# Half of a tuned kernel's first layer by seven half-size products in place of eight

## The chip, the cores and the metric

The kernel runs on 1 core of one Trainium2 chip. The metric is the device time of one execution in microseconds (us), median over several runs. The ratios are of runs in the undisturbed state ("fast"), in which the profiler shows 0.992 to 1.0 of TensorE's clock granted.

## The reference

Sliding-window attention (8 batches, 8 heads, 576 positions, head size 64, window 32 to each side), then a two-layer network with a gelu over 4608 tokens:

```python
scores = scale * np.matmul(q, k.transpose(0, 1, 3, 2))
mask = np.abs(pos[:, None] - pos[None, :]) <= 32
attn = softmax(np.where(mask, scores, -1e9))          # cut: written out in the reference
x = np.matmul(attn, v) ...                            # to 4608 x 512
h = x @ w_in                                          # 512 -> 2048
g = h * (1.0 / (1.0 + np.exp(-1.702 * h)))
return (g @ w_out).astype(np.float32)                 # 2048 -> 512
```

## The kernel before

Tokens are worked off in windows of 256. In window w the kernel does attention for its tokens, the first layer for those of window w-1 and the second layer for those of window w-2. Windows 0 to 3 are the head, 4 and 5 lead in, 6 to 17 are alike, 18 and 19 close. The second layer is done already by a product of 2 x 2 blocks with seven block products in place of eight (Strassen's scheme in Winograd's form): VectorE makes the sums of g (`g_sums`) and keeps partial results (`keep`, `result`), TensorE does seven `product`s of 8 matmuls.

The first layer is plain: for each pair of 128-column blocks of w_in, 8 matmuls with 256 tokens as the moving operand, then a gelu on ScalarE.

```python
def layer1(self, t, d, kind="h"):
    hps = self.bank(kind, [128, 2, 256], F32, "h_ps")
    ffs = (d, d + 8) if t > 2 else (2 * d, 2 * d + 1)
    for i in range(2):
        ff = ffs[i]
        for kr in range(self.NK):
            nc.tensor.matmul(hps[:, i, :], self.w_in_sb[:, kr, ff * 128:(ff + 1) * 128], self.xT[t][:, kr, :], ...)
    nc.scalar.activation(self.g[t][:, ffs[0]:ffs[1] + 1:ffs[1] - ffs[0], :], hps, AF.Gelu_apprx_sigmoid)

def window(self, w):                     # cut to the order for w > 5; t = w - 2
    self.scores(a); self.scores(b)
    self.g_sums(t, 1, (0, 1)); self.product(t, 1, "o"); self.keep(t, 1, dve)
    self.product(t, 2, "h"); self.g_sums(t, 1, (2, 3)); self.result(t, 11)
    self.product(t, 5, "t"); self.band(a); self.product(t, 6); self.band(b, 0); self.keep(t, 6, dve); self.band(b, 1)
    run(l1)                              # one layer1
    self.values(a); self.values(b); self.norm(a); self.x_T(a)
    self.product(t, 7); self.keep(t, 7, dve); self.result(t, 22); run(l1, 1)
    self.product(t, 4); self.result(t, 21, act); self.norm(b); self.x_T(b)
    self.product(t, 3); self.result(t, 12)
    run(l1, 2); self.g_sums(w - 1, 0); self.feed(w); run(l1, 4)
```

In the head, vo copies (shifted copies of v that the values need) stand ahead of the masks:

```python
for m in range(4, 7):
    self.odd_v(m, dve)
self.band(4)
```

The softmax here doesn't subtract the row's maximum and nothing guards it: scores larger than these inputs give would overflow.

## Time and profile before

| | before |
|---|---|
| time, median of the first 3 runs | 291.88 us (291.85 to 293.37) |
| TensorE busy | 283.1 us, 98% of the span |
| VectorE, ScalarE busy | 190.5 (66%), 183.3 (63%) |
| one window | 14.57 us |
| VectorE, ScalarE busy in a window | 10.13 to 10.4, 9.87 |

How to read the lines that follow: PE is TensorE, PEld its weight loads, DVE VectorE, ACT ScalarE. A line of the chain of waits is a start and a length in us, the engine, the tile that it writes, the line of the kernel and how many instructions. The tiles are `sc` (scores), `p` (their exponentials), `ve` and `vo` (v and its shifted copies), `pv` (values), `x` (normed values), `tp` (transposes), `h_ps` (plain first layer), `h_main` and `h_side` (the two banks of the seven products, new in the change), `xs` and `wi_sum` (the sums of x and of w_in, also new), `g` (after the gelu), `gs` (sums of g), `o_ps` (second layer), `part` and `o_sb` (its partial and finished results). A bank is one of the pieces of memory in which this kernel's matmuls leave their results. A bracket at the end of a timeline line is the time that the engine stood idle before it, and what ended that.

Read the chain of waits first: the column of starts gives the length of a window, and the names tell that only TensorE stands in it from 46 us until the last results at 284.4. Then ask of the chain's pieces what they are made of, and of VectorE and ScalarE how much room a window leaves them. The prediction shows the lines.

### The profile page before, as it was taken

How to read it: one execution, taken by the hardware profiler on the slowest of the kernel's cores; microseconds unless marked ns; L12 is line 12 of the kernel's file. 1: busy time of each engine (PE TensorE's matmuls, PEld its weight loads, DVE VectorE, ACT ScalarE, POOL GpSimd, SP SyncE). 2: the span in 40 equal slices, each digit the busy share in tenths (PEclk: the TensorE clock that was granted, in tenths of full speed). 3: DMA queues.
4: the chain of work that ended last, by engine and by line, in shares of the span. 5: the costliest groups of instructions: out<-in, count | busy, mean ns of one | idle time of the engine just before them, and what ended most of it. 6: DMA issues, size and time to landing. Idle time of an engine off the chain costs nothing.

```text
span 289.8 us, 9011 instructions
## 1 busy us (share of the span) xinstructions
PE 283.1 (98%) x3757; PEld 233.7 (81%) x3759; DVE 190.5 (66%) x563; ACT 183.3 (63%) x301; POOL 101.7 (35%) x140
## 2 busy tenths in 40 slices
PE   7989999999999999999999999999999999999995
PEld 2668655866888888888888888888888888888884
DVE  6871558679576767676767685858585858583352
ACT  4576366695757676767666666767676767675330
POOL 8854425997635443442524343422000000000000
PEclk9999999999999999999999999999999999999999
DMA  9999999999999999999999999999925220312012
GB/s 152 189 200 205 199 183 161 165 138 150 176 141 151 157 193 139 160 157 162 154 181 111 154 133 160 130 159 137 152 57 147 36 93 20 95 21 91 2 72 72
DMA packets 144824, 38.79 MB, mean 134 GB/s; under 512 B 129936, under 2 KB 140432, under 8 KB 144784
## 3 DMA queue, kind: packets, MB, share of 16 engines
q0 software_dynamic: 97232, 18.16, 85.3%
q1 hardware_dynamic: 47104, 19.67, 38.9%
q8 instruction: 29, 0.48, 0.7%
q10 hardware_dynamic: 448, 0.39, 0.5%
q14 instruction: 11, 0.09, 0.2%
HBM read 36.96 MB, written 9.44 MB: 160 GB/s over the span
## 4 chain that ended last, share of the span: by engine, by line
PE 82%; DMA 12%; POOL 3%; DVE 1%; issue 1%; ACT 0%; POOLq 0%; DVEq 0%
PE h_ps L339 39%; PE o_ps L401 32%; DMA ks<-in_k_dram 5%; DMA ve<-in_v_dram 4%; PE o_ps L351 4%; PE pv L299 4%; PE sc L270 3%; DMA w_in_sb<-in_moe_w_in_dram 3%; POOL ve L159 1%; PE tp L178 1%; POOL ks L137 0%; POOL ks L197 0%; POOL qs L197 0%; PE tp L326 0%; DVE o_sb L419 0%
## 5 line engine op out<-in xcount | busy, mean ns | idle before, releaser
L339 PE MATMUL h_ps<-xT,w_in_sb 128*128 128x256 bf16 x1152 | 134.9, 273 | 0.0
L341 ACT ACTIVATE g<-h_ps 128x512 f16<-128x512 f32 x144 | 85.6, 595 | 73.3 <-PE h_ps L339 72.0
L339 PEld LDWEIGHTS <-w_in_sb 128*128 128x128 bf16 x1152 | 112.1, 98 | 13.4
L159 POOL DMA_DIRECT2D ve<-in_v_dram x41 | 34.4, 849 | 76.2 <-PE pv L299 56.8
L401 PEld LDWEIGHTS <-gs 128*128 128x128 f16 x480 | 45.8, 98 | 5.8
L401 PE MATMUL o_ps<-w_sum,gs 128*128 128x256 f16 x360 | 44.3, 273 | 0.0
L277 ACT ACTIVATE p<-sc 128x512 bf16<-128x512 f32 x72 | 37.2, 604 | 3.8 <-PE sc L270 3.6
L378 DVE TENSOR_TENSOR gs<-g 128x512 f16<-128x512 f16 x30 | 12.8, 425 | 38.5 <-ACT g L341 38.5
L401 PEld LDWEIGHTS <-g 128*128 128x128 f16 x360 | 34.2, 98 | 4.5 <-ACT g L341 0.2
L311 DVE TENSOR_TENSOR x<-pv,rec 128x256 bf16<-128x256 f32 x72 | 30.6, 424 | 2.5
L401 PE MATMUL o_ps<-w_out_sb,g 128*128 128x256 f16 x240 | 29.1, 273 | 0.0
L105 DVE COPY part<-o_ps 128x256 f32<-128x256 f32 x45 | 19.1, 424 | 12.2 <-PE o_ps L401 11.1
L419 DVE TENSOR_TENSOR o_sb<-o_ps,part 128x256 f32<-128x256 f32 x45 | 19.0, 422 | 12.1 <-PE o_ps L401 11.4
L105 DVE COPY vo<-ve 64x528 bf16<-64x528 bf16 x71 | 22.6, 318 | 6.0 <-DMA ve<-in_v_dram 4.4
L288 DVE TENSOR_TENSOR p<-p,mask 128x512 bf16<-128x512 bf16 x64 | 24.6, 425 | 0.7 <-ACT p L277 0.6
L147 POOL DMA_DIRECT2D qs<-in_q_dram x27 | 22.8, 868 | 5.9 <-DMA ks<-in_k_dram 4.8
L147 POOL DMA_DIRECT2D ks<-in_k_dram x27 | 22.8, 858 | 2.7 <-DMA ve<-in_v_dram 1.5
L351 PE MATMUL o_ps<-w_out_sb,g 128*128 128x512 f16 x96 | 23.2, 380 | 0.0
L438 ACT ACT_TABLE_LOAD x15 | 19.2, 1283 | 0.3
L277 ACT ACT_TABLE_LOAD x15 | 19.2, 1283 | 0.3
L310 DVE RECIPROCAL rec<-pv 128x4 f32<-128x4 f32 x72 | 12.5, 174 | 6.2 <-PE pv L299 6.2
L299 PEld LDWEIGHTS <-p 128*64 128x64 bf16 x576 | 11.1, 110 | 6.2 <-DVE p L288 3.9
(79 smaller groups left out, 237.0 us busy)
## 6 DMA issues: line engine op xcount, KB each, us to landing
out_dram<-o_sb SPq DMA_DIRECT2D x34, 256.0 KB, 4.4
ve<-in_v_dram POOLq DMA_DIRECT2D x31, 128.0 KB, 6.1
ks<-in_k_dram POOLq DMA_DIRECT2D x24, 128.0 KB, 7.1
qs<-in_q_dram POOLq DMA_DIRECT2D x24, 128.0 KB, 8.5
w_in_sb<-in_moe_w_in_dram POOLq DMA_DIRECT2D x4, 512.0 KB, 9.2
w_out_sb<-in_moe_w_out_dram POOLq DMA_DIRECT2D x4, 512.0 KB, 14.1
ve<-in_v_dram POOLq DMA_DIRECT2D x10, 64.0 KB, 6.1
ks<-in_k_dram POOLq DMA_DIRECT2D x7, 64.0 KB, 6.0
```

The source lines that it names most:

```text
L105: (eng.copy if eng is self.nc.scalar else eng.tensor_copy)(out, in_)
L147: self.nc.gpsimd.dma_start(self.stage[key][off:off + m, n], src[b, :, s:s + m, :].rearrange("h s d -> s h d"))
L159: self.nc.gpsimd.dma_start(self.ve[m % NV][lo + off:lo + off + n, :, :self.D], self.v[b, :, s:s + n, :].rearrange("h s d -> s h d"))
L277: nc.scalar.activation(p[:, eo], sc[eo], AF.Exp, scale=self.scale)
L288: self.nc.vector.tensor_mul(pv, pv, msk.to_broadcast([128, 4, 2, SQ]))
L299: nc.tensor.matmul(acc[half][blk * 64:blk * 64 + 64, hh, :], p[:, h % 2, h // 2 * 2 + blk, :], vt[:, h, :D + 1], start=(hh == 0), stop=(hh ...
L311: nc.vector.tensor_mul(x[:, hs, :], acc[half][:, :, :D], rec[:, hs, :].to_broadcast([128, 4, D]))
L339: nc.tensor.matmul(hps[:, i, :], self.w_in_sb[:, kr, ff * 128:(ff + 1) * 128], self.xT[t][:, kr, :], start=(i == 0 and kr == 0), stop=(i = ...
L341: nc.scalar.activation(self.g[t][:, ffs[0]:ffs[1] + 1:ffs[1] - ffs[0], :], hps, AF.Gelu_apprx_sigmoid)
L351: nc.tensor.matmul(o_ps, self.g[t][:, ff, s * 128:(s + 1) * 128], self.w_out_sb[:, ff, :], start=(ff == 0), stop=(ff == self.NFF - 1))
L401: nc.tensor.matmul(self.part[t, key], x, y, start=(first and k == 0), stop=(k == 7), skip_group_check=True)
L438: self.nc.scalar.activation(self.spark, self.spark, AF.Gelu_apprx_sigmoid)
```

## The change

The intent is to save matmul columns in the first layer by the scheme that the second layer has. Half of it (column blocks 4 to 7 and 12 to 15) is cut in 2 x 2 blocks, and eight block products become seven, each of 8 matmuls of 128 columns. The operands become f16, since sums of them are taken. The price is sums of x per window, sums of w_in once, and moves between banks, on VectorE and ScalarE. The second layer's sums are placed anew around the masks, pairs of banks are joined so that one mask, one exponential or one norm serves both halves, and a few orders and buffers move.

```diff
+    def w_in_sums(self):                  # once, in window 5
+        dve.tensor_add(ws[:, 0], w[:, top, v], w[:, low, v])
+        dve.tensor_sub(ws[:, 1], ws[:, 0], w[:, top, u])
+        dve.tensor_sub(ws[:, 2], w[:, top, u], w[:, top, v])
+        dve.tensor_sub(ws[:, 3], w[:, low, u], ws[:, 1])
+    def seven(self, t, n):                # 4 blocks x 2 matmuls of 128 columns; cut
+        dst = hs["main" if n in (1, 6, 5, 3) else "side"]
+    def steady(self, w):                  # windows 6 to 17; t = w - 1, o = w - 2; loads and gelu_table cut
+        self.scores(a, which=0); self.scores(b, which=1)
+        self.g_sums(o, 1, (0, 1)); self.product(o, 1, "o"); self.keep(o, 1, dve)
+        self.g_sums(o, 0, (2,)); self.product(o, 2, "t"); self.result(o, 11)      # if w > 6
+        self.product(o, 6); self.band(a); self.keep(o, 6, dve); self.product(o, 5, "t"); self.band(b)
+        self.g_sums(o, 1, (2,)); self.seven(t, 1); self.move("side", "main", dve); self.x_sums(t, (0, 1))
+        self.values(a, which=0); self.values(b, which=1); self.norm(a); self.x_T(a)
+        self.product(o, 7); self.keep(o, 7, dve); self.result(o, 22); self.x_sums(t, (2, 3)); self.norm(b); self.x_T(b)
+        ...                               # two g_sums
+        self.seven(t, 2); self.gelu(t, "side", 0, 0); self.seven(t, 6); self.move("k2", "main", act)
+        self.layer1(t, 0, "a"); self.product(o, 4); self.result(o, 21, act)
+        self.seven(t, 7); self.move("k7", "side", act); self.seven(t, 5); self.move("22", "main", dve, "k7")
+        self.feed(w); self.layer1(t, 1, "b"); self.gelu(t, "22", 1, 1); self.layer1(t, 2, "b"); self.layer1(t, 3, "a")
+        self.seven(t, 4); self.move("21", "side", dve, "k2"); self.seven(t, 3)
+        self.gelu(t, "main", 0, 1); self.gelu(t, "21", 1, 0)
+        self.g_sums(t, 0, (0, 1)); self.product(o, 3); self.result(o, 12)
@@ window
-        if w > 5:
-            self.scores(b)
-        self.product(t, 2, "h")
-        if w == 5:
-            self.scores(b)
+        self.product(t, 2, "h")
+        self.scores(b, which=1)
         self.feed(w)
+        self.w_in_sums()
         run(l1, 4)
@@ head
-        self.keep_busy(2, "h")
+        self.keep_busy(2, "o")            # fillers ahead of scores 2
-        for m in range(4, 7):
+        for m in range(4, 6):
             self.odd_v(m, dve)
         self.norm(4)
+        self.odd_v(6, dve)
-        o_sb ... bufs=4
+        o_sb ... bufs=3
```

More of the change, by code (lines that the diff above doesn't have):

```diff
@@ L59, in __init__, with pair, halves @@
         self.gs, self.part, self.o_sb = {}, {}, {}
+        self.xs, self.hs, self.turn = {}, {}, 0
     def bank(self, kind, shape, dtype, name):
-        bufs = {"h": 2, "o": 1, "a": 4, "t": 1}[kind]
+        bufs = {"h": 2, "o": 1, "t": 1, "b": 2}[kind]
         return self.ps.tile(shape, dtype, name=name, tag=kind, bufs=bufs)
+    def pair(self, name, which=None):
+        if which is None:
+            which, self.turn = self.turn, 1 - self.turn
+        if which == 0:
+            return self.ps.tile([128, 2, 512], F32, name=name, tag="a", bufs=1)
+        return [self.bank("b", [128, 512], F32, f"{name}{i}") for i in range(2)]
+    @staticmethod
+    def halves(pair):
+        return pair if isinstance(pair, list) else [pair[:, i] for i in range(2)]
     def setup(self):
@@ L69, in setup @@
         self.mask = cst.tile([128, 4, SQ], BF16, name="mask")
-        self.w_in_sb = cst.tile([128, self.NK, self.DFF], BF16, name="w_in_sb")
+        self.w_in_sb = cst.tile([128, self.NK, self.DFF], F16, name="w_in_sb")
+        self.wi_sum = cst.tile([128, 4, 2, self.DFF // 4], F16, name="wi_sum")
+        self.ident16 = cst.tile([128, 128], F16, name="ident16")
         self.w_out_sb = cst.tile([128, self.NFF, self.DM], F16, name="w_out_sb")
@@ L214, in load_raw @@
         lo, size = self.tokens("A")
-        raw = self.stage[c, "raw", hp] = self.cst.tile([size // JT, 2, JT * self.D], F32, name=f"{c}_raw{hp}")
+        if "raw" not in self.stage:
+            self.stage["raw"] = self.work.tile([128, 4, 2, JT * self.D], F32, name="raw", tag="gs")
+        raw = self.stage[c, "raw", hp] = self.stage["raw"][:size // JT, 2 * hp + "kq".index(c)]
         src = {"q": self.q, "k": self.k}[c]
@@ L248, in blind, with scores @@
     def blind(self, u):
-        sc = self.sc[u] = [self.bank("a", [128, 8, SQ], F32, f"sc{eo}") for eo in range(2)]
+        sc = self.sc[u] = self.pair("sc")
         neg = self.neg.rearrange("k (o b) s -> k o b s", o=1).to_broadcast([128, 4, 2, SQ])
         for eo in range(2):
-            self.nc.tensor.matmul(sc[eo].rearrange("k (h b) s -> k h b s", b=2), self.ident, neg,
+            self.nc.tensor.matmul(self.halves(sc)[eo].rearrange("k (h b s) -> k h b s", b=2, s=SQ), self.ident, neg,
                                   start=True, stop=False, skip_group_check=True)
-    def scores(self, u):
+    def scores(self, u, which=None):
         nc = self.nc
@@ L259, in scores @@
         if seen:
-            self.sc[u] = [self.bank("a", [128, 8, SQ], F32, f"sc{eo}") for eo in range(2)]
-        sc = self.sc.pop(u)
+            self.sc[u] = self.pair("sc", which)
+        both = self.sc.pop(u)
+        sc = [half.rearrange("k (h s) -> k h s", s=SQ) for half in self.halves(both)]
         k0, q0 = 128 * u % RING, (128 * u + 32) % RING
@@ L275, in scores, with band @@
         p = self.work.tile([128, 2, 8, SQ], BF16, name="p", tag="p", bufs=5)
-        for eo in range(2):
-            nc.scalar.activation(p[:, eo], sc[eo], AF.Exp, scale=self.scale)
+        if isinstance(both, list):
+            for eo in range(2):
+                nc.scalar.activation(p[:, eo], sc[eo], AF.Exp, scale=self.scale)
+        else:
+            nc.scalar.activation(p.rearrange("k e h s -> k e (h s)"), both, AF.Exp, scale=self.scale)
         self.p[u] = p
-    def band(self, u, only=None):
+    def band(self, u):
         p = self.p[u]
@@ L284, in band, with values @@
         a, b = 0 if cross[0] else 1, 2 if cross[1] else 3
-        for eo in range(2) if only is None else (only,):
-            pv = p[:, eo].rearrange("p (h b) s -> p h b s", b=2)
-            msk = self.mask[:, a:b + 1:b - a, :].rearrange("p (o b) s -> p o b s", o=1)
-            self.nc.vector.tensor_mul(pv, pv, msk.to_broadcast([128, 4, 2, SQ]))
-    def values(self, u, kinds="aa"):
+        pv = p.rearrange("p e (h b) s -> p (e h) b s", b=2)
+        msk = self.mask[:, a:b + 1:b - a, :].rearrange("p (o b) s -> p o b s", o=1)
+        self.nc.vector.tensor_mul(pv, pv, msk.to_broadcast([128, 8, 2, SQ]))
+    def values(self, u, kinds=None, which=None):
         nc, D = self.nc, self.D
         p = self.p.pop(u)
-        acc = [self.bank(kinds[i], [128, 4, D + 1], F32, f"pv{i}") for i in range(2)]
+        if kinds is None:
+            both = self.pair("pv", which)
+            acc = [half[:, :4 * (D + 1)].rearrange("q (h d) -> q h d", d=D + 1) for half in self.halves(both)]
+            if isinstance(both, list):
+                self.acc[u] = acc
+            else:
+                self.acc[u] = [both[:, :, :4 * (D + 1)].rearrange("q i (h d) -> q i h d", d=D + 1)]
+        else:
+            acc = self.acc[u] = [self.bank(kinds[i], [128, 4, D + 1], F32, f"pv{i}") for i in range(2)]
         for half in range(2):
@@ L300, in values @@
                                      vt[:, h, :D + 1], start=(hh == 0), stop=(hh == 3))
-        self.acc[u] = acc
     def norm(self, u):
@@ L305, in norm @@
         acc = self.acc.pop(u)
-        x = self.work.tile([128, self.H, D], BF16, name="x", tag="x", bufs=4)
+        x = self.work.tile([128, self.H, D], F16, name="x", tag="x", bufs=4)
         rec = self.work.tile([128, self.H, 1], F32, name="rec", tag="rec", bufs=3)
+        if len(acc) == 1:
+            rec4 = rec.rearrange("q (i h) o -> q i h o", i=2)
+            nc.vector.reciprocal(rec4, acc[0][:, :, :, D:D + 1])
+            nc.vector.tensor_mul(x.rearrange("q (i h) d -> q i h d", i=2), acc[0][:, :, :, :D],
+                                 rec4.to_broadcast([128, 2, 4, D]))
+            self.x[u] = x
+            return
         for half in range(2):
@@ L317, in x_T @@
         if s == 0:
-            self.xT[t] = self.work.tile([128, self.NK, 256], BF16, name="xT", tag="xT", bufs=4)
+            self.xT[t] = self.work.tile([128, self.NK, 256], F16, name="xT", tag="xT", bufs=4)
         x = self.x.pop(u)
@@ L323, in x_T @@
             return
-        tp = self.bank(kind, [128, 4, 128], BF16, "tp")
+        tp = self.bank(kind, [128, 4, 128], F16, "tp")
         for c in range(4):
-            nc.tensor.transpose(tp[:, c, :], x[:, 2 * c:2 * c + 2, :], self.ident)
+            nc.tensor.transpose(tp[:, c, :], x[:, 2 * c:2 * c + 2, :], self.ident16)
         self.cast(eng or nc.vector, out, tp)
@@ L331, in layer1 @@
         nc = self.nc
-        if d == 0:
+        if t not in self.g:
             self.g[t] = self.work.tile([128, self.NFF, 256], F16, name="g", tag="g", bufs=2)
-        hps = self.bank(kind, [128, 2, 256], F32, "h_ps")
+        if kind == "a":
+            hps = self.pair("h_ps", 0)[:, 0].rearrange("p (i s) -> p i s", i=2)
+        else:
+            hps = self.bank(kind, [128, 2, 256], F32, "h_ps")
         ffs = (d, d + 8) if t > 2 else (2 * d, 2 * d + 1)
@@ L353, in layer2 @@
         if quarter == 3:
-            o_sb = self.work.tile([128, self.DM], F32, name="o_sb", tag="o_sb", bufs=4)
+            o_sb = self.work.tile([128, self.DM], F32, name="o_sb", tag="o_sb", bufs=3)
             self.cast(eng or nc.vector, o_sb, o_ps)
@@ L412, in result @@
         if u not in self.o_sb:
-            self.o_sb[u] = self.work.tile([128, self.DM], F32, name="o_sb", tag="o_sb", bufs=4)
+            self.o_sb[u] = self.work.tile([128, self.DM], F32, name="o_sb", tag="o_sb", bufs=3)
         cols = slice(256 * half, 256 * half + 256)
@@ L438, in gelu_table, with keep_busy @@
         self.nc.scalar.activation(self.spark, self.spark, AF.Gelu_apprx_sigmoid)
-    def keep_busy(self, n, kind="a"):
+    def keep_busy(self, n, kind="b"):
         junk = self.bank(kind, [128, 512], F32, "junk")
@@ L456, in head @@
         self.setup_neg()
+        dve.tensor_copy(self.ident16, self.ident)
         for m in range(2):
@@ L498, in head @@
         self.keep_busy(2, "o")
-        self.values(1, "oa")
+        self.values(1, "ob")
         self.norm(1)
@@ L513, in head @@
         self.layer1(0, 1)
-        self.values(2)
+        self.values(2, which=1)
         self.norm(2)
-        self.values(3)
+        self.values(3, which=0)
         self.norm(3)
         self.x_T(2, "t")
-        self.layer1(0, 2, "a")
+        self.layer1(0, 2, "b")
         self.x_T(3, "o")
@@ L541, in head @@
         for hp in range(4):
-            self.rows_T("k", 1, hp, "a", dve)
-            self.rows_T("q", 1, hp, "a", act)
+            self.rows_T("k", 1, hp, "b", dve)
+            self.rows_T("q", 1, hp, "b", act)
             run(1)
@@ L561, in head @@
         run(1)
-        self.x_T(4, "a", act)
+        self.x_T(4, "b", act)
         run(1)
-        self.x_T(5, "a", act)
+        self.x_T(5, "b", act)
         run(1)
@@ L580, in head @@
             self.layer1(2, d)
-        self.x_T(6, "a")
+        self.x_T(6, "b")
         self.layer1(2, 3)
@@ L596, in head, with x_sums @@
             self.rows_X(c, 3, (0, 1))
+    def w_in_sums(self):
+        w, ws, dve = self.w_in_sb, self.wi_sum, self.nc.vector
+        top, low, u, v = slice(0, 2), slice(2, 4), slice(512, 1024), slice(1536, 2048)
+        dve.tensor_add(ws[:, 0], w[:, top, v], w[:, low, v])
+        dve.tensor_sub(ws[:, 1], ws[:, 0], w[:, top, u])
+        dve.tensor_sub(ws[:, 2], w[:, top, u], w[:, top, v])
+        dve.tensor_sub(ws[:, 3], w[:, low, u], ws[:, 1])
+    def x_sums(self, t, which):
+        dve, x = self.nc.vector, self.xT[t]
+        xs = self.xs[t]
+        top, low, u, v = slice(0, 2), slice(2, 4), slice(0, 128), slice(128, 256)
+        for n in which:
+            p, m = [(x[:, top, v], x[:, top, u]), (x[:, low, v], xs[:, 0]),
+                    (x[:, low, v], x[:, top, v]), (x[:, low, u], xs[:, 1])][n]
+            dve.tensor_sub(xs[:, n], p, m)
@@ new lines, in seven @@
+    def seven(self, t, n):
+        hs = self.hs
+        if n == 1:
+            self.xs[t] = self.work.tile([128, 4, 2, 128], F16, name="xs", tag="xs", bufs=1)
+            self.g[t] = self.work.tile([128, self.NFF, 256], F16, name="g", tag="g", bufs=2)
+            hs["main"], hs["side"] = (self.bank("h", [128, 4, 128], F32, name) for name in ("h_main", "h_side"))
+        x, xs, w, ws = self.xT[t], self.xs[t], self.w_in_sb, self.wi_sum
+        dst = hs["main" if n in (1, 6, 5, 3) else "side"]
+        u, v = slice(0, 128), slice(128, 256)
+        for f in range(4):
+            here = slice(128 * f, 128 * f + 128)
+            top, low = slice(512 + 128 * f, 640 + 128 * f), slice(1536 + 128 * f, 1664 + 128 * f)
+            for k in range(2):
+                a, b = {1: (w[:, k, top], x[:, k, u]), 2: (w[:, 2 + k, top], x[:, 2 + k, u]),
+                        3: (ws[:, 3, k, here], x[:, 2 + k, v]), 4: (w[:, 2 + k, low], xs[:, 3, k]),
+                        5: (ws[:, 0, k, here], xs[:, 0, k]), 6: (ws[:, 1, k, here], xs[:, 1, k]),
+                        7: (ws[:, 2, k, here], xs[:, 2, k])}[n]
+                self.nc.tensor.matmul(dst[:, f], a, b, start=(n in (1, 7) and f == 0 and k == 0),
+                                      stop=(f == 3 and k == 1), skip_group_check=True)
@@ new lines, in move, with gelu @@
+    def move(self, key, src, eng, add=None):
+        if key != "side":
+            self.hs[key] = self.work.tile([128, 2, 4, 128], F32, name="hs", tag="kc" if key[0] == "k" else "qc")[:, 0]
+        if add is None:
+            self.cast(eng, self.hs[key], self.hs[src])
+        else:
+            self.nc.vector.tensor_add(self.hs[key], self.hs[src], self.hs[add])
+    def gelu(self, t, src, low, v):
+        at = 12 if low else 4
+        self.nc.scalar.activation(self.g[t][:, at:at + 4, 128 * v:128 * v + 128], self.hs[src], AF.Gelu_apprx_sigmoid)
@@ new lines, in loads @@
+    def loads(self, w):
+        for m in (2 * w + 6, 2 * w + 7):
+            if m < self.NU:
+                self.load_v(m)
+        i, chunks = w // 2 + 2, ((0, 1), (2, 3))[w % 2]
+        if 512 * i < self.N:
+            for c in "kq":
+                self.load_rows(c, i, chunks)
+    def steady(self, w):
+        dve, act = self.nc.vector, self.nc.scalar
+        a, b, t, o = 2 * w, 2 * w + 1, w - 1, w - 2
+        self.loads(w)
+        self.scores(a, which=0)
+        self.scores(b, which=1)
+        self.g_sums(o, 1, (0, 1))
+        self.product(o, 1, "o")
+        self.keep(o, 1, dve)
+        if w > 6:
+            self.g_sums(o, 0, (2,))
+        self.product(o, 2, "t")
+        self.result(o, 11)
+        self.gelu_table()
+        self.product(o, 6)
+        self.band(a)
+        self.keep(o, 6, dve)
+        self.product(o, 5, "t")
+        self.band(b)
+        self.g_sums(o, 1, (2,))
+        self.seven(t, 1)
+        self.move("side", "main", dve)
+        self.x_sums(t, (0, 1))
+        self.values(a, which=0)
+        self.values(b, which=1)
+        self.norm(a)
+        self.x_T(a)
+        self.product(o, 7)
+        self.keep(o, 7, dve)
+        self.result(o, 22)
+        self.x_sums(t, (2, 3))
+        self.norm(b)
+        self.x_T(b)
+        if w > 6:
+            self.g_sums(o, 0, (3,))
+        self.g_sums(o, 1, (3,))
+        self.seven(t, 2)
+        self.gelu(t, "side", 0, 0)
+        self.seven(t, 6)
+        self.move("k2", "main", act)
+        self.layer1(t, 0, "a")
+        self.product(o, 4)
+        self.result(o, 21, act)
+        self.seven(t, 7)
+        self.move("k7", "side", act)
+        self.seven(t, 5)
+        self.move("22", "main", dve, "k7")
+        self.feed(w)
+        self.layer1(t, 1, "b")
+        self.gelu(t, "22", 1, 1)
+        self.layer1(t, 2, "b")
+        self.layer1(t, 3, "a")
+        self.seven(t, 4)
+        self.move("21", "side", dve, "k2")
+        self.seven(t, 3)
+        self.gelu(t, "main", 0, 1)
+        self.gelu(t, "21", 1, 0)
+        self.g_sums(t, 0, (0, 1))
+        self.product(o, 3)
+        self.result(o, 12)
@@ L607, in run @@
                 lst.pop(0)()
-        def loads():
-            for m in (2 * w + 6, 2 * w + 7):
-                if m < self.NU:
-                    self.load_v(m)
-            i, chunks = w // 2 + 2, ((0, 1), (2, 3))[w % 2]
-            if 512 * i < self.N:
-                for c in "kq":
-                    self.load_rows(c, i, chunks)
         if w == 4:
@@ L640, in window @@
             run(l2)
-            loads()
+            self.loads(w)
             for m in (10, 11):
@@ L647, in window @@
             return
-        loads()
+        self.loads(w)
         if not att:
@@ L651, in window @@
             return
-        self.scores(a)
-        if w > 5:
-            self.scores(b)
+        self.scores(a, which=0)
         self.g_sums(t, 1, (0, 1))
@@ L658, in window @@
         self.product(t, 2, "h")
-        if w == 5:
-            self.scores(b)
+        self.scores(b, which=1)
         self.g_sums(t, 1, (2, 3))
@@ L666, in window @@
         self.product(t, 6)
-        self.band(b, 0)
         self.keep(t, 6, dve)
-        self.band(b, 1)
+        self.band(b)
         run(l1)
-        self.values(a)
-        self.values(b)
+        self.values(a, which=0)
+        self.values(b, which=1)
         self.norm(a)
@@ L693, in close @@
         last = not l1
+        if not last:
+            self.g_sums(t, 0, (2, 3))
         self.g_sums(t, 1, (0, 1))
-        for n, kind in ((1, "o"), (2, "a"), (6, None), (5, "a"), (7, None)):
+        for n, kind in ((1, "o"), (2, "b"), (6, None), (5, "b"), (7, None)):
             self.product(t, n, kind)
@@ L718, in close @@
             dve.tensor_add(both, self.part[t, "c"], self.part[t, 6])
-            self.product(t, 3, "a")
+            self.product(t, 3, "b")
             self.part[t, 6], self.part[t, "c"] = both, self.part[t, "d"]
@@ L744, in run @@
         for w in range(4, self.NW + 2):
-            self.window(w)
+            self.steady(w) if 5 < w < self.NW else self.window(w)
 @with_exitstack
```

## The prediction

> **What bounds the kernel now.** I read the engine totals first, then the chain that ended last, then the groups, then the timeline of one steady stretch. The totals and the chain's shares:
>
> ```profile
> PE 283.1 (98%) x3757; PEld 233.7 (81%) x3759; DVE 190.5 (66%) x563; ACT 183.3 (63%) x301; POOL 101.7 (35%) x140
> PEclk9999999999999999999999999999999999999999
> PE 82%; DMA 12%; POOL 3%; DVE 1%; issue 1%; ACT 0%; POOLq 0%; DVEq 0%
> ```
>
> TensorE is busy all the time at full clock. A busy PE need not be useful, so I look at what the chain is made of. One whole window (256 tokens) of it, up to the next window's scores:
>
> ```profile
> 91.70 0.63 PE sc L270 x32
> 92.32 3.60 PE o_ps L401 x32
> 95.92 0.87 PE h_ps L339 x8
> 96.80 0.63 PE pv L299 x32
> 97.43 0.98 PE o_ps L401 x8
> 98.41 0.87 PE h_ps L339 x8
> 99.28 1.75 PE o_ps L401 x16
> 101.03 5.24 PE h_ps L339 x48
> 106.27 0.63 PE sc L270 x32
> ```
>
> The window is 106.27 - 91.70 = 14.57 us, and the same figures come again in every window to the end. There are no waits in it: 64 first-layer matmuls of 256 columns take 6.98 (0.109 each), 56 second-layer ones 6.33, scores and values 0.63 each. The kernel is bound by matmul columns, and only fewer columns, or the head before 45 us, can shorten it.
>
> The next question is what a 128-column matmul costs when every one has new weights. The kernel has some, the transposes:
>
> ```profile
> 55.05 0.45 PE tp L178 x8
> L326 PE MATMUL tp<-ident,x 128*128 128x128 bf16 x32 | 3.1, 220 | 0.6 <-DVE x L311 0.6
> L326 PEld LDWEIGHTS <-x 128*128 128x128 bf16 x32 | 2.2, 98 | 1.7 <-DVE x L311 0.9
> ```
>
> Eight take 0.45 us, 0.056 each, with a load before each. So halving the columns halves the time (0.109 to 0.056); the load does not show.
>
> The durations that I use for VectorE and ScalarE:
>
> ```profile
> L378 DVE TENSOR_TENSOR gs<-g 128x512 f16<-128x512 f16 x30 | 12.8, 425 | 38.5 <-ACT g L341 38.5
> L311 DVE TENSOR_TENSOR x<-pv,rec 128x256 bf16<-128x256 f32 x72 | 30.6, 424 | 2.5
> L366 DVE TENSOR_TENSOR w_sum<-w_out_sb 128x1024 f16<-128x1024 f16 x4 | 2.7, 684 | 5.3 <-DMA w_out_sb<-in_moe_w_out_dram 5.3
> L105 DVE COPY o_sb<-o_ps 128x512 f32<-128x512 f32 x3 | 2.1, 686 | 1.3 <-PE o_ps L351 1.2
> L105 ACT COPY o_sb<-o_ps 128x512 f32<-128x512 f32 x3 | 1.7, 580 | 0.6 <-PE o_ps L351 0.6
> ```
>
> **What the Trainium skill says.** "TensorE: Matmul & The Clock Gate", Back-to-back issue gap, gives two figures for 128 columns: N/2.4 + 2.5 ns (56) for isolated matmuls, and about 81 ns for streams of load and matmul. The trace has such pairs at 56, though only in runs of 8; I take it, and keep 81 as a rival. "VectorE: DVE Perf Modes", The perf-mode tier table, has tensor_tensor at two elements a cycle for 16-bit operands in SBUF and one with any in PSUM. The trace agrees: 512 f16 elements take 425 ns, 256 from PSUM 424. "PSUM — Partial Sum Buffer", Engine vs sequencer instructions, calls VectorE's and ScalarE's queues strict FIFO. The trace agrees: at 44.56 a vo copy had waited 2.28 us for a transfer, and the mask multiply behind it, whose exponentials began at 42.10, came only then.
>
> **The change part by part.** It is in the 12 windows 6 to 17.
>
> *TensorE.* Blocks 4-7 and 12-15 of the first layer, 32 matmuls of 256 columns, 32 x 0.109 = 3.49 us, become 7 products x 8 matmuls of 128 columns: 56 x 0.056 = 3.14 (I use 3.12, at 55.8 ns). The gain is 0.37 per window, 12 x 0.37 = 4.4 us. That is nearly all there is to win, 1.5%.
>
> *VectorE* does 10.3 us per window now (busy time of 91.7:106.3 by engine). Added: four x sums of 256 f16 elements, from the slope between 425 (512) and 684 (1024) about 0.295 each, 1.18; three moves or adds of 512 f32 elements from PSUM, 0.69 each, 2.07. Taken away: the two masks of a unit become one of 1024, four times 0.425 to twice 0.69, 0.32; the first norm becomes one reciprocal and one multiply, 2 x (0.17+0.42) to 0.18+0.69, 0.31. The sum is 12.9 of 14.2 us, 91%.
>
> *ScalarE* does 9.87 now; two copies of 512 columns add 1.16, the joined exponential saves about 0.1 (slope of the copies, 372 to 580 for 256 to 512): 10.9, 77%.
>
> Neither sum passes 14.2, so the order decides. I laid the new order out from the window's start, with PE times as above, 0.2 us from the end of a stream to its reader (matmuls' ends lie 0.17 behind their issue, and readers start 0.04 later), 0.1 lost after scores and after values as now (3.60 for 32, 0.98 for 8):
> - The last gelu of the old window ends at about 0.4, table load to 1.7, exponentials done at 2.8 and 3.8. VectorE: result 12 until 0.7, sums 0 and 1 until 1.5, copy of product 1 (ends 1.8) until 2.2; product 6 wants it at 2.5. Masks end at 3.7 and 4.65; values want them at 4.67 and 4.99. Here is the least slack, some 0.3.
> - Product 1 of the seven ends at 4.67: move to the side bank until 5.6, two x sums until 6.1, norm until 6.94. The next user of that bank, a plain layer-1 group, comes at 7.18.
> - Copy of product 7 to 7.3, result 22 to 7.6, x sums to 8.1 (wanted at 8.92), second norm to 9.2 (9.82), two sums to 9.9, add of product 5 (ends 10.0, its copy by ScalarE 10.2) to 10.9, vo copies to 12.2. Then VectorE waits until 13.1.
>
> So every result is there in time, with 0.2 to 0.3 to spare, and TensorE stays the bound: 14.57 - 0.37 = 14.2.
>
> *Where time is lost.* In window 5 the four sums of w_in (1024 elements each: 0.69 + 0.61 + 0.61 + 0.69 with a dependence or two, 2.6 us) stand on VectorE after the vo copies. Those ended at 91.88 now (from 90.44, 1.44 long), 0.2 after window 6's scores. So the sums end 2.8 into window 6; then two second-layer sums and the copy of product 1 until 3.95, and product 6, wanted at 2.5, waits: 1.5 us, once.
>
> *The head.* The vo copy that waited for the late v block is moved behind two masks:
>
> ```profile
> 44.56 0.29 DVE L105 COPY vo<-ve 64x528 bf16<-64x528 bf16 x1 [2.28 <-DMA ve<-in_v_dram]
> 45.57 0.30 PEld L299 LDWEIGHTS <-p 128*64 128x64 bf16 x14 [0.23 <-DVE p L288]
> ```
>
> Second-layer work ran out about 45.05 and values went on at 45.57, so about 0.4 comes back. The new bank layout of the head and the filler's bank move 0.1 either way.
>
> Sum: 291.9 - 4.4 + 1.5 - 0.4 = 288.6.
>
> *The store.* Output buffers go from 4 to 3, and the store of result 12 now stands behind four transposes on its queue (6 to 7 us of issue now, e.g. 176.03 to 182.87). It would be issued about 3.1 into the next window and land 4.4 later (median for stores), near 7.6 to 8. Result 22, which takes that buffer, is due at 7.2. VectorE may stand still 0.5 there; the x sum behind it is due at 8.92, so it costs nothing or 0.1. I put 0.1 us in all into the number.
>
> **Rivals.**
> 1. *Weight loads show.* At 81 ns the 56 matmuls take 4.5 us, 1.05 more than the 32: 12 x 1.05 = 12.6, near 305. For: a load is recorded as 98 ns[...]; runs here are 8 or 16. Against: the transposes at 56 in the same kernel. Break-even is 62 ns.
> 2. *VectorE becomes the bound*, by its load of 91% or by a late store. If each of 12 windows loses 0.3, the gain is gone: 292. For: the slack of 0.2, the FIFO order, a copy from PSUM to PSUM whose cost no row shows. Against: VectorE idles from 12.2 to 13.1, so a lag is made good within a window.
> 3. *No stall in window 6*, since the sums might start earlier: 287.1. Against: they stand behind copies that end at 91.88 and nothing else is moved.
>
> **Range and chances.** The gain cannot be much above 4.4 + 0.4, which gives 287.0; noise of the runs is 1.5 upward (291.85 to 293.37). Rival 2 in part gives up to 292. So 288.7, range 286.7 to 292.0. Faster by over 2% needs under 286.0, for which I see no source: 0.06. Slower by over 2%, over 297.7, takes rival 1 or a heavy rival 2: 0.08. Within 2%: 0.86.
>
> **What would show it.** Right: windows 14.2 us long from window 7 on, a chain still of PE alone, 8 matmuls of the seven in 0.45, VectorE near 12.9 per window, window 6 about 1.5 longer with product 6 waiting for a VectorE copy behind w_in sums. Wrong: 8 of the seven taking 0.65; PE idle in each window released by a mask, norm or x sum; a DVE wait on a store longer than 1 us; no wait in window 6.

## The result, and the profile after

| | before | after |
|---|---|---|
| time, median of 4 runs each | 292.24 us | 288.65 us (288.06 to 290.18) |
| ratio, 95% interval | | 0.9879 (0.9831 to 0.9927) |
| TensorE busy | 283.1 | 278.5 |
| VectorE busy | 190.5 | 216.6 |
| one window | 14.57 | 14.21 |
| VectorE, ScalarE busy in a window | 10.13 to 10.4, 9.87 | 12.2 to 12.8, 10.73 |

A ratio is the mean time of one kernel's fast runs over that of the other's fast runs of the same rounds, so it isn't quite the ratio of the medians. By the 2% measure the two kernels are the same; the interval lies wholly below 1.

The totals and the shares of the chain in the changed kernel:

```profile
PE 278.5 (97%) x4045; PEld 234.4 (82%) x4047; DVE 216.6 (76%) x586; ACT 193.3 (67%) x307; POOL 102.2 (36%) x140
PE 65%; DVE 1%; ACT 0%; issue 0%; DVEq 0%
```

The shares add up to 66% because the chain could be followed back only to 95.2 us, a wait which is read below; from there on it is TensorE, as before. One window of it, up to the scores of the next:

```profile
107.13 0.63 PE sc L287 x32
107.76 3.60 PE o_ps L437 x32
111.36 0.45 PE h_main L673 x8
111.80 0.63 PE pv L326 x32
112.44 0.98 PE o_ps L437 x8
113.42 0.45 PE h_side L673 x8
...
121.33 0.63 PE sc L287 x32
```

121.33 - 107.13 = 14.20, with no waits, and 8 matmuls of the seven take 0.45. The groups of new work, from the list with shapes apart (busy time, then mean ns of one):

```profile
L673 PE MATMUL h_main<-xs,wi_sum 128*128 128x128 f16 x192 | 14.6, 219 | 0.0
L119 DVE COPY h_side<-h_main 128x512 f32<-128x512 f32 x12 | 8.3, 695 | 0.0
L653 DVE TENSOR_TENSOR xs<-xT 128x256 f16<-128x256 f16 x24 | 6.8, 282 | 0.0
```

Where the time went, by starts of the same work on TensorE:

| | before | after | after less before |
|---|---|---|---|
| scores 4 (head) | 40.96 | 41.13 | +0.17 |
| scores 6 (head) | 45.92 | 45.69 | -0.23 |
| window 5 | 76.82 | 76.59 | -0.23 |
| window 6 | 91.63 | 91.45 | -0.18 |
| window 7 | 106.27 | 107.13 | +0.86 |
| window 17 | 252.14 | 249.20 | -2.94 |
| window 18 | 266.77 | 263.41 | -3.36 |
| end of the span | 289.8 | 286.4 | -3.4 |

(Window 7 on is from the chain, whose starts are some 0.06 later than the engine's own in both kernels.) Eleven windows gain 4.2 together. The head gains 0.2, the close nothing. Window 6 loses 1.04, its own gain of 0.37 included: 1.41 of it are new. The timeline shows what that is:

```profile
91.45 0.68 DVE L640 TENSOR_TENSOR wi_sum<-w_in_sb 128x1024 f16<-128x1024 f16 x1
...
93.37 0.69 DVE L643 TENSOR_TENSOR wi_sum<-w_in_sb,wi_sum 128x1024 f16<-128x1024 f16 x1
...
94.77 0.42 DVE L119 COPY part<-o_ps 128x256 f32<-128x256 f32 x1
95.24 1.91 PE L437 MATMUL o_ps<-w_sum,gs 128*128 128x256 f16 x16 [1.24 <-DVE part L119]
```

The w_in sums begin with window 6 and hold VectorE's queue until 94.06; then come two sums of g and the copy of product 1, for which product 6 has waited 1.24 us (1.41 from the issue of the matmul before it, as a matmul's recorded end lies 0.17 behind: x8 are 1.04 long in the timeline and 0.87 in the chain).

### The profile page after: what moved, and what is told of

It is laid out like the page before. It is cut to its first block, busy times and chain, and to the rows that moved or that the text cites. A ratio compares the mean times of both kernels' runs of the same rounds, so it can differ in the third digit from the quotient of the medians.

```text
span 286.4 us, 9622 instructions
## 1 busy us (share of the span) xinstructions
PE 278.5 (97%) x4045; PEld 234.4 (82%) x4047; DVE 216.6 (76%) x586; ACT 193.3 (67%) x307; POOL 102.2 (36%) x140
## 4 chain that ended last, share of the span: by engine, by line
PE 65%; DVE 1%; ACT 0%; issue 0%; DVEq 0%
PE o_ps L437 30%; PE h_ps L375 17%; PE h_main L673 7%; PE h_side L673 6%; PE pv L326 3%; PE sc L287 2%; DVE o_sb L455 0%; DVE part L119 0%; ACT o_sb L119 0%; DVE part L872 0%; DVEq L455 0%
## 5 line engine op out<-in xcount | busy, mean ns | idle before, releaser
L375 PE MATMUL h_ps<-xT,w_in_sb 128*128 128x256 f16 x768 | 91.1, 273 | 0.0
L375 PEld LDWEIGHTS <-w_in_sb 128*128 128x128 f16 x768 | 73.6, 98 | 8.7 <-DMA w_in_sb<-in_moe_w_in_dram 0.2
L377 ACT ACTIVATE g<-h_ps 128x512 f16<-128x512 f32 x96 | 57.1, 596 | 34.6 <-PE h_ps L375 32.9
L119 DVE COPY vo<-ve 64x528 bf16<-64x528 bf16 x71 | 23.3, 329 | 4.5 <-DMA ve<-in_v_dram 2.7
L307 DVE TENSOR_TENSOR p<-p,mask 128x1024 bf16<-128x1024 bf16 x32 | 22.1, 693 | 2.7 <-ACT p L297 2.3
L673 PEld LDWEIGHTS <-wi_sum 128*128 128x128 f16 x384 | 23.5, 98 | 0.3
L688 ACT ACTIVATE g<-h_side 128x512 f16<-128x512 f32 x12 | 7.2, 597 | 21.0 <-PE h_side L673 11.6
L295 ACT ACTIVATE p<-sc 128x512 bf16<-128x512 f32 x36 | 19.5, 597 | 1.9 <-PE sc L287 1.9
L673 PEld LDWEIGHTS <-w_in_sb 128*128 128x128 f16 x288 | 19.1, 98 | 0.8
L297 ACT ACTIVATE p<-sc 128x1024 bf16<-128x1024 f32 x18 | 18.5, 1025 | 1.6 <-PE sc L287 1.4
```

What stands on the lines that cost most here:

```text
L119: (eng.copy if eng is self.nc.scalar else eng.tensor_copy)(out, in_)
L295: nc.scalar.activation(p[:, eo], sc[eo], AF.Exp, scale=self.scale)
L297: nc.scalar.activation(p.rearrange("k e h s -> k e (h s)"), both, AF.Exp, scale=self.scale)
L307: self.nc.vector.tensor_mul(pv, pv, msk.to_broadcast([128, 8, 2, SQ]))
L673: self.nc.tensor.matmul(dst[:, f], a, b, start=(n in (1, 7) and f == 0 and k == 0), stop=(f == 3 and k == 1), skip_group_check=True)
```

## The experiments

All are made from the changed kernel except e11, and all gave correct results. Each was run beside the kernel before; "after" means the changed kernel of the result above.

**e1: the w_in sums in the head.**

```diff
+        self.w_in_sums()                  # head, ahead of w_sums
         for n in range(4):
             self.w_sums(n, 0)
@@ window
         self.feed(w)
-        self.w_in_sums()
```

> The four sums of w_in are made in the head, where VectorE is idle, in place of window 5. My theory: window 6 loses 1.4 us in the changed kernel (boundaries 91.45 to 107.06 against 14.21 in the windows after it) only because these sums stand ahead of the copy of product 1; so window 6 shrinks to 14.2, PE shows no wait there, and the time falls by 1.4 to about 287.2. Rival: the first window of the new kind loses time for another reason (first use of the banks, the changed order of sums), then window 6 stays near 15.6 and the time near 288.6. A second rival: the sums wait in the head for a late load of w_in and hold the queue there, then the head grows by some tenths and about 288 results.

Measured: 287.47 us against 292.39, ratio 0.9851 (0.9814 to 0.9887); after had 0.9879. The chain of waits in e1, window 6 and the next two:

```profile
91.49 0.63 PE sc L287 x32
...
105.72 0.63 PE sc L287 x32
...
119.93 0.63 PE sc L287 x32
```

Window 6 is 14.23 long and the wait of product 6 is gone from the list of TensorE's waits. In the head the sums ran from 24.9 to 27.5, after 2.87 us in which VectorE waited for w_in, and ended before the w_out data for the rest of its work was there (30.2): they cost nothing there (scores 6 start at 45.66, in after at 45.69). The first rival falls; of the second the wait for w_in came true, but not its cost. The intervals of e1 and after overlap, so it is the trace that shows the 1.4, not the times alone.

**e2: the old window everywhere.**

```diff
-            self.steady(w) if 5 < w < self.NW else self.window(w)
+            self.window(w)
```
(and no w_in sums)

> The changed kernel with the old window in all windows: no seven products, no w_in sums, but the joined masks and norms, the new banks, f16 operands and the head of the changed kernel. My theory: the seven products alone bring the gain of 0.37 per window, so windows return to 14.57 and the time to that of before less the head's 0.2 to 0.4, 291.6. Rival: the joined masks and norms and the reordered sums bring a part; then windows lie between 14.2 and 14.57 and the time below 290.5.

Measured: 295.86 us against 292.39, ratio 1.0131 (1.0091 to 1.0171). Both expectations failed: it is slower than before, with windows of 14.86. The chain:

```profile
151.60 1.85 PE o_ps L437 x16
153.45 0.38 PE sc L287 x16
153.82 1.85 PE o_ps L437 x16
```

The edit was not what I took it for. In the changed kernel's `window`, the second scores stand behind product 2 in every window, where before had that in window 5 alone. So TensorE goes to scores twice.

**e10: as e2, with both scores at the start.**

```diff
         self.scores(a, which=0)
+        if w > 5:
+            self.scores(b, which=1)
@@
-        self.scores(b, which=1)
+        if w == 5:
+            self.scores(b, which=1)
```

> As e2, but with both scores at the window's start, as in before (in e2 the second scores stand behind product 2 in every window, which the edit had overlooked). My theory: the 0.28 that e2's windows were longer than those of before (14.86 to 14.57) is only this split, so windows return to 14.57, and with them the time to that of before less 0 to 0.4. Rival: the joined masks and norms and the new banks cost the 0.28, then windows stay at 14.86 and the time 3 us above before. Second rival: they bring something, then under 14.5.

Measured: 292.58 us against 292.47, ratio 1.0002 (0.998 to 1.0024); windows of 14.63:

```profile
107.07 0.63 PE sc L287 x32
112.17 0.69 PE pv L326 x32
121.70 0.63 PE sc L287 x32
```

So the joined masks and norms, the banks and the f16 operands bring nothing by themselves (0.06 per window the other way, all of it in the values: 0.69 in place of 0.63), though they take VectorE from 10.15 to 9.8 us per window. The window of the new kind gains from the seven products. Its new order is no rival: without waits in either chain, the pieces that both windows have take the same (second layer 6.33 before and 6.32 after, scores and values 0.63 each, the plain matmuls that stayed 3.49), and only 3.49 of the first layer has become seven times 0.45. And the split of the scores alone cost 14.86 - 14.63 = 0.23 per window.

**e3: early sums, and window 5 in the new form too.**

```diff
-            self.steady(w) if 5 < w < self.NW else self.window(w)
+            self.steady(w) if 4 < w < self.NW else self.window(w)
```
(on top of e1, and the two `if w > 6` ahead of second-layer sums become `if w > 5`)

> As e1, and window 5 also runs in the new form (13 windows in place of 12), which only the early sums allow. My theory: each window of the new form is worth 0.37, and window 5 loses another 0.2 now by scores in two places: 287.2 - 0.6 = 286.6. Rival: the first new window meets gelu or sums of window 4 in another order and stalls, then about 287.2 or more.

Measured: 286.81 us (286.17 to 287.64) against 292.39, ratio 0.9809 (0.9781 to 0.9837). Window 5 is 90.77 - 76.53 = 14.24 long in place of 14.86 in after (91.45 - 76.59). By its trace this is the fastest version (span 284.6 us, after 286.4), though its interval and that of after still overlap by a little. Two of its windows took 14.4: the one from 105.05 lost 0.2 between product 2 and product 6, the one from 133.69 lost 0.2 within product 7 (8 matmuls at 138.93 took 1.25 in place of 1.05). I found no cause for that in the trace, and it stays open.

**e4: the third vo copy back ahead of the masks.**

```diff
-        for m in range(4, 6):
+        for m in range(4, 7):
             self.odd_v(m, dve)
@@
         self.norm(4)
-        self.odd_v(6, dve)
```

> The changed kernel with the third vo copy of the head put back ahead of the two masks. My theory: the copy waits for a late v block and holds the masks, so values 4 end 0.4 later after scores 4 (in before the second-layer matmuls behind values 4 started 5.34 after scores 4, in the changed kernel 4.94), and the time is 0.2 to 0.4 longer, 289.0. Rival: the 0.4 came of the joined masks (two 1024 multiplies in place of four), then the distance stays near 4.94 and the time at 288.6.

Measured: 289.32 us, ratio 0.989 (0.9859 to 0.9921), no different from after. From scores 4 to scores 6 it took 4.56 as in after, not longer. But in this run scores 4 came at 42.01, 0.9 later than in after (TensorE had waited 0.7 for a piece of w_in), while the v block was there at 44.60, as in before; so the copy held the masks for less, and values 4 were ready in time. The run does not decide the question, and e11 was made for it.

**e11: the kernel before, with only that copy moved.**

```diff
-        for m in range(4, 7):
+        for m in range(4, 6):
             self.odd_v(m, dve)
@@
         self.norm(4)
+        self.odd_v(6, dve)
```

> The kernel before with nothing changed but the third vo copy of the head, moved behind norm 4. My theory: the masks no longer wait for the v block, the distance from scores 4 to scores 6 falls from 4.96 to 4.56 and the time by up to 0.4, which the spread of the runs may hide. Rival: values 4 wait anyway, for exponentials or the masks, and the distance stays near 4.96.

Measured: 291.84 us against 292.47, ratio 0.9987 (0.996 to 1.0014), which tells nothing. The trace does: from scores 4 (41.16) to scores 6 (45.73) it is 4.57 in place of 4.96, and the mask waits for its exponential, no longer for the copy:

```profile
43.00 1.82 DVE L288 TENSOR_TENSOR p<-p,mask 128x512 bf16<-128x512 bf16 x4 [0.83 <-ACT p L277]
```

So the move is worth 0.39 us in a run in which the v block comes as late as in the profile of before, and nothing in one like e4's.

**e5 and e6: needless work on VectorE in two places.** Two additions in each of the 12 new windows, in e5 ahead of the first norm:

```diff
         self.values(b, which=1)
+        for _ in range(2):
+            dve.tensor_add(self.idle, self.idle, self.idle)
         self.norm(a)
```

In e6 the same two lines stand behind `self.feed(w)`, that is, behind the vo copies.

> Two needless additions of 512 bf16 elements on VectorE (0.42 each, about 0.8 of the queue together) in each of the 12 new windows, just ahead of the first norm. My theory: the order decides. The norm ends 0.2 ahead of the layer-1 group that takes its bank, so TensorE waits about 0.6 in each window: windows 14.8, time 288.6 + 12 x 0.6 = 295.8. Rival: only the sum of VectorE's work counts, and 12.4 + 0.8 is under 14.2, so nothing is lost: 288.6.

> The same two additions in the same windows, but behind the vo copies, where VectorE waits 0.3 to 0.9 for the last but one product. My theory: nearly all of it falls into that wait, windows stay at 14.2 to 14.3 and the time at 288.6 to 289.5. Rival: VectorE is close enough to its limit for 0.8 us to show anywhere, then 14.8 per window and 295.8 as in the other place.

Measured for e5: 296.73 us against 291.83, ratio 1.0177 (1.014 to 1.0213), windows of 14.83, which is 0.62 more than 14.21. For e6: 288.94 against 291.83, ratio 0.9916 (0.988 to 0.9951), windows of 14.21. Of e5 the list of TensorE's waits (total, times, longest):

```profile
PE h_ps L375 <- DVE x L337: 5.4, 12, 0.5
```

Of e6 the timeline of VectorE: the additions fill the gap, and the next piece follows at once.

```profile
119.23 0.87 DVE L750 TENSOR_TENSOR idle<-idle 128x512 bf16<-128x512 bf16 x2
120.08 0.69 DVE L683 TENSOR_TENSOR hs<-h_side,hs 128x512 f32<-128x512 f32 x1
```

The same 0.87 us (0.88 in e5) cost 0.62 in one place and nothing in the other. The rival by which only VectorE's total counts falls: the order decides.

**e7: 128-column matmuls where the changed kernel has 256.**

```diff
+            if 5 <= t < self.NW - 1:          # the plain half in the new windows
+                for kr in range(self.NK):
+                    for s in range(2):
+                        cols = slice(128 * s, 128 * s + 128)
+                        nc.tensor.matmul(hps[:, i, cols], w_in block, self.xT[t][:, kr, cols], ...)
```

> The plain half of the first layer in the 12 new windows with 128-column matmuls: 64 of 128 columns in place of 32 of 256, each with its own weight load; the same work otherwise. My theory: a 128-column matmul with a load costs 0.056, so a window grows by 64 x 0.056 - 32 x 0.109 = 0.1 at most and the time by 1, to 289.7. Rival: loads show in longer runs of 16 to 48 (0.081 a matmul): 64 x 0.081 - 3.49 = 1.7 per window, 309.

Measured: 290.1 us against 291.83, ratio 0.9936 (0.9913 to 0.996); windows of 14.29, 0.08 more than in after. 64 matmuls of 128 columns with 64 weight loads replace 32 of 256: (3.49 + 0.08) / 64 = 0.056 each, in runs of up to 48. The longest run in the chain:

```profile
117.91 2.68 PE h_ps L378 x48
```

The weight load does not show; halving the columns costs 1 ns per half. (The rival's 0.081 is the 81 ns of the Trainium skill that the prediction cites.)

**e9: two output buffers in place of three.** Four, as before, did not fit into the memory.

```diff
-            o_sb ... bufs=3
+            o_sb ... bufs=2
```

> Output buffers 2 in place of 3 (4 do not fit into the memory). My theory: with 3 the buffer of result 22 comes free just in time, its store being issued 3.3 us into the window and landing about 3.6 later, at 6.9, with result 22 at 7.05. With 2, result 11, due at 2.4, needs that store, so VectorE stands until 6.9 in windows 7 to 17, product 5 behind it: some 3.5 us per window where transposes stand ahead of the store (windows 7 to 15), 288.6 + 9 x 3.5 = 320. Rival: stores land much earlier than that, then the cost is under 1 us per window, below 300.

Measured: 291.7 us (290.63 to 295.97) against 291.83, ratio 0.998 (0.995 to 1.0011); the run of 295.97 is slow, and the ratio is of the other three. My expectation of 320 was far off. In the 12 windows VectorE waits for a store at six results, for 0.22 to 1.11 us: twice at result 22 and four times at result 11. The first of each:

```profile
115.64 0.42 DVE L455 TENSOR_TENSOR o_sb<-o_ps,part 128x256 f32<-128x256 f32 x1 [0.58 <-DMA out_dram<-o_sb]
125.67 0.42 DVE L455 TENSOR_TENSOR o_sb<-o_ps,part 128x256 f32<-128x256 f32 x1 [1.11 <-DMA out_dram<-o_sb]
```

The first is result 22 of window 7. It takes here the buffer whose store stands behind the transposes (issued at 111.10, when result 11 had begun already at 110.46; landed 4.4 later). The second is result 11 of window 8, which starts at 122.08. It waits for the other store, that of result 21 of window 7, issued at 118.87 and landed 6.7 later. So the two results take the buffers the other way round from what I had thought. The wait of 0.58 cost TensorE nothing (that window is 14.20 long); that of 1.11 cost 0.83 (15.04), and those at result 11 in windows 9, 10 and 12 cost 0.44, 0.30 and 0.19. The rest of e9's loss came before window 7, which starts 0.8 later than in after; 0.48 of it is a wait of TensorE at 53.28 behind ScalarE, which had itself waited 1.82 for a store. With three buffers no wait of VectorE for a store is in the list at all.

## Why the prediction was right

It said 288.7 us and 288.65 was measured; it gave 0.86 to a change within 2%. The near hit owes something to luck: single runs spread over 2 us, and errors of 0.1 to 0.2 in the terms partly offset each other. Step by step:

- *The bound and the gain of 0.37.* Right. Windows are 14.21 as against 14.2 predicted, the chain is of TensorE alone, 8 of the seven take 0.45. e10 shows that nothing else in the window gives the gain, e7 that the price of 0.056 holds in long runs. Rival 1 (81 ns) falls. Rival 2 (VectorE) did not come about: from window 7 on the list of TensorE's waits has none for VectorE.
- *The order on VectorE.* Right in substance. The tight places in the trace of after are those named:

```profile
151.40 0.43 DVE L119 COPY part<-o_ps 128x256 f32<-128x256 f32 x1 [0.32 <-PE o_ps L437]
152.07 1.91 PE L437 MATMUL o_ps<-w_sum,gs 128*128 128x256 f16 x16
155.84 0.69 DVE L337 TENSOR_TENSOR x<-pv,rec 128x512 f16<-128x512 f32 x1
156.77 1.04 PE L375 MATMUL h_ps<-xT,w_in_sb 128*128 128x256 f16 x8
```

  The copy ends at 151.83, 0.24 ahead of product 6, and the norm at 156.53, 0.24 ahead of the group that takes its bank. e5 took that slack away and the loss followed: 0.62, which is 0.87 less the 0.24. The masks had a little more room than I gave them (the first ended at 153.29, 1.1 ahead of the values that read it, the second at 154.22, 0.4 ahead; I had 1.0 and 0.3).
- *VectorE's sum.* Too high: 12.9 predicted, 12.2 to 12.8 measured. I added mean durations, while the busy time counts an overlap of neighbours once: an instruction of 0.43 is followed by the next after 0.34 where that does not depend on it (151.40 and 151.74 in the window above).
- *Window 6.* Right: 1.5 predicted, 1.41 measured, the sums ending 2.6 into the window rather than 2.8. e1 shows the cause. Rival 3 falls.
- *The head.* Right in the mechanism, wrong in the net: "about 0.4 comes back" is what e11 measured (0.39), and after passes from +0.17 to -0.23 between scores 4 and scores 6. The +0.17 comes from earlier: in that run a v block landed later, the vo copy waited until 17.22 in place of 16.77, and the values of units 2 and 3 with it. That is another run's transfers, not the change, as far as one profile each can tell; e4's head was 0.9 late in the same way. The filler's new bank shows no gain: from the filled bank ahead of it to scores 2 it is 1.20 us before (14.32 to 15.52) and 1.26 after (14.10 to 15.36).
- *The store.* This step failed: "Result 22, which takes that buffer". With three buffers it doesn't take that one: in window 7 of after, result 22 begins at 114.27 without a wait, while that store, issued at 111.28, lands 5.9 later. The 0.1 I put in for it was for a wait that doesn't exist. The time computed for the wait was good all the same: in e9, where result 22 does take it, VectorE waited in window 7 until 7.76 into the window (115.64 - 107.88), against the 7.6 to 8 predicted.

So the sum of the terms, -4.4 + 1.5 - 0.4 + 0.1, became in the trace -4.6 (the eleven windows' 4.2 and window 6's own 0.37), +1.4, -0.2 and 0. The windows' term is 0.2 above mine because in before a few windows lost 0.1 at the scores: the eleven of before average (266.77 - 106.27) / 11 = 14.59.

## What to carry to other kernels

Where a chain of waits is made of matmuls alone, count columns: seven products for eight gain what the columns say, as long as every sum reaches its reader, and that is decided by the place of each instruction in its engine's queue, not by the engine's busy share. One-time preparation belongs where its engine waits for something anyway; here 2.6 us of it cost 1.4 in the pipelined part and nothing in the head. When an experiment switches a part off by an existing branch, check that branch against the old kernel line by line first.

## What the Trainium skill lacked or had wrong

- "TensorE: Matmul & The Clock Gate", Back-to-back issue gap, says of streams of weight load and matmul that they sustain about 81 ns at 128 columns. In e7 runs of up to 48 such pairs took 56 ns each, which is the page's figure for isolated matmuls.
- No page gives a figure for the cost of going from scores or values (64-row or 64-column tiles) to full products: 32 products behind scores take 3.60 against 32 x 0.109 = 3.49, 8 behind values 0.98 against 0.87, and splitting the scores in two cost 0.23 per window (e2 against e10).
- "VectorE: DVE Perf Modes", The perf-mode tier table, has one column for any operand in PSUM and no row for PSUM to PSUM. A copy of 512 f32 elements from bank to bank took 695 ns, as one from PSUM to SBUF did (686).
- "PSUM — Partial Sum Buffer", The four PSUM rules, says that a matmul without the first flag adds onto what VectorE wrote where the bit is set, and calls 0 the only seed that is safe whether it is set or not. The side bank is seeded by a VectorE copy of product 1 here and accumulated onto in 12 windows, with correct results in every kernel here that has the seven products, so a nonzero seed worked. That doesn't contradict the page if earlier matmuls in the same bank had left the bits set; this is my reading of the page, and no run tests it.
